# A dilated-convolution kernel: one written-out order of work replaced by another, with accumulating transfers placed differently around the loads

## The chip, the cores and the metric

The kernel runs on one core of one Trainium2 chip. The core has a matrix engine (PE, whose weight loads are listed as PEld), a vector engine (DVE), an activation engine (ACT), a general engine (POOL) and a synchronising engine (SP). SP and POOL also issue transfers, which run on 16 DMA engines. Each engine works through its own instructions in the order in which they were written and waits on semaphores for the others. The metric is the device time of one execution in microseconds (us).

## The reference

The input `x` has shape (2, 16000, 256). A causal convolution with three taps and dilation 2 makes 512 channels, the first 256 go through tanh, the other 256 through a sigmoid, their product is multiplied by a 256 x 256 matrix:

```
xp = jnp.pad(x, ((0, 0), (pad, 0), (0, 0)))          # pad = 4
h = einsum(xp[:, 4:4 + T], w[0])
for i in 1, 2:
    h = h + einsum(xp[:, 4 - 2*i : 4 - 2*i + T], w[i])
z = jnp.tanh(h[..., :256]) * sigmoid(h[..., 256:])
return z @ w_o
```

All inputs are bfloat16, as is the output (2, 16000, 256).

## The kernel before, in words

**Tiling.** Time is cut into 23 groups: one of kind P at the very beginning, 18 of kind A (6 time phases x 256 rows) and four of kind B (4 phases x 256 rows, the last of them 160 rows). A group is loaded by one transposing DMA (line 167, issued by SP), so that channels lie on the partitions. Of each group, four blocks of 128 output channels are worked out (`oi` 0 to 3). ORDER gives the sequence of the groups: three of kind B, then A, with the 160-row group last.

**The fast convolution.** Instead of three products for each output, an A group makes six output phases, two at a time, from five products, whose inputs are sums and differences of the phases. These inputs ("pre-sums") are made per group, 128 x 1024 elements each: `u0`, `u1`, `u2`, `e`, `f` from the loaded tile, `u3`, `uh`, `ud` as scaled copies of `u1`, and finally four that are added on top of one of those: `rp = f + u1`, `rm = e + u3`, `r0 = u0 + uh`, `ri = u2 + ud`. A B group needs only `m`, `p`, `d0`, `d3`. The weights are transformed to match; the pieces of the matrix `wa_sb` are made on POOL (line 233) in 16 steps, `wa.0` to `wa.15`: the first eight add into `wu`, the last eight write `wa_sb`. `wa.8` and `wa.12` serve block 0 of a group, `wa.10` and `wa.14` block 1, `wa.9` and `wa.13` block 2, `wa.11` and `wa.15` block 3; each needs the step numbered eight lower (`wa.9` needs `wa.1`, `wa.13` needs `wa.5`).

**Three ways to make a pre-sum.** On DVE in one piece (line 330 or 328); on POOL in four quarters (line 330, 128 x 256 each); or, for `rp`, `rm`, `r0`, `ri`, by a DMA that POOL issues (line 325) and that adds its source into its destination. Nearly all of those four kinds go by such an accumulating DMA, 67 in all.

**The order.** PLAN is a list of tokens, and each token writes one step; since each engine keeps its own order, the list sets the order on every engine at once.
- `F`, `M`, `L`, `Z`, `I`: the five products of the next block (line 359, two matmuls of 512 columns each): `F` uses `u1`, `M` uses `rm`, `L` uses `rp`, `Z` uses `r0`, `I` uses `ri` (for B groups `m`, `p`, `d0`, `d3`, and no `M`). `P` is the output product of one piece (line 478, four matmuls of 256 columns). `H` and `R` are its two halves for the last pieces. I call these, with the three `D`, the PE tokens.
- `c` copies the first product to SBUF on ACT (line 390). Behind `M` the second product is taken out of the accumulating bank by `h` (DVE, line 393) or by `k` (ACT, line 403). `A` and `Y` are combining sums on DVE (line 393). `b`, `y`, `a` are tanh or sigmoid on ACT (line 441), `g` the gate product on DVE (line 460).
- `e` and `v` take an output piece out of PSUM, on ACT (line 495) or DVE (line 487); `s` stores (line 504) and `x` loads the next group (line 167), both through SP's queue, in the list's order.
- `u1.3` makes that pre-sum of the fourth A group (they count from 0) on DVE; `u1.3q5` makes one quarter on POOL, held until the DVE step that was the fifth last at this point is done; `r0.3d` issues the accumulating DMA.

The first three groups (12 blocks) are of kind B, so the thirteenth `F`, the thirteenth `L`, the thirteenth `Z` and the first `M` belong to the first A group. Four loads are issued ahead of the list (lines 534 to 537), so the third `x` is the seventh load.

Of the kernel before, what the change touches and what calls it, by code (L numbers as in the profile page):

```python
# [40 lines left out]
f.8 e.7q127 c Z I Y y M b A rm.7d P a ud.8 rp.7d F k26 uh.7 Z u0.7 c I g y L r0.7d b M u2.7q72 A P a F k27 u3.8
u2.7q63 P Y e44 L c u1.9 ri.7d s17 I e45 s16 e.9 Z y x M A b P f.9 k28 P Y a F L e46 u2.8 Z e47 g I b u0.9q178 P c A
F e48 uh.8 M u0.9q158 c Y P a u0.9q136 h29 M y Z u0.8q109 h30 s18 I b rm.8d g L a L r0.8d y A F u0.9q4 e49 P Y I c
u3.9 Z a u1.10q52 A M b u2.9q181 Y I k31 F rm.9d uh.9 e50 e.10 Z c s19 L rp.8 b s6 P f.10q126 A x y M a F Y u2.9q45
P e51 h32 u2.9q161 Z c g u1.10q99 L b I y Y M y u1.10q83 F A a P u1.10q114 h33 c Z ri.8 rp.9d L b M ud.9 r0.9d y Y F
k34 I uh.10 u1.11q50 c A L a M v52 u1.11q37 e53 Z A f.10q162 k35 I y P Y u2.9q165 L a g x P e54 f.11q189 Z b A I e55
f.10q170 v56 F b P ri.9d Y c P u3.10 a F g s20 rm.10d y M s21 Z c h36 I e57 u0.10 M b L u2.10 a r0.10d F A k37 P
f.10q70 e58 Y L y P f.11q62 A c Z rp.10d ud.10 y P Y I ri.10d b u0.11 M e59 Z a h38 s22 F b x g L u1.12q10 c I e60 Y
M y P A u1.11q150 e61 F h39 u1.12q153 e62 Z e.11 c f.11q86 L I a Y M b u1.11q185 A P a f.11q166 F h40 y Z rp.11d
u3.11 c P uh.11 e63 rm.11d L f.12 b M g e64 I P k41 A u2.12q76 F a Y L u1.12q230 y I A c u2.12q102 Z a P u1.12q84 Y  # L50
b M u0.12 r0.11d e65 Z g rp.12d k42 F s24 I y s23 ud.11 L c u2.11 P b M e.12 ri.11d e66 P A k43 u1.13q10 F a v67 P
e68 L Y u1.13q109 c P A u1.13q60 Z e69 M e.13q198 e70 Y I b u2.12q181 h44 Z y F ud.12 a uh.12 L u3.12 c r0.12d P g b
M rm.12d e71 I Y u2.12q118 k45 F s26 A a P x u2.13 L c e.13q58 Z y A M b u1.13q162 I Y e72 F u0.13q202 h46 y P
ri.12d c f.13 Z a L u3.13 M u1.14 b P y A e.14q169 I k47 s25 g F e.13q265 e73 I a Y L c P e.13q147 A e74 Z u0.13q254
y M Y rm.13d P b uh.13 P h48 e75 rp.13d Z a ud.13 F f.14 b ri.13d L c g I e76 F u2.14q57 Y e77 M c P A s28 e.14q54 P
y x h49 u0.13q177 M a Z uh.14 u2.14q98 y h50 L b I u2.14q236 A y L e.14q154 Y a F P u2.14q72 e78 Y Z c u0.13q9 A I y
v80 M r0.13d b s27 I g e79 F k51 Z ud.14 c P e.15 a L u0.14 M b f.15q17 A P a P u3.14 k52 f.15q94 Y F e81 L e.14q63
v83 c Z y rp.14d A M b I g k53 P u2.15q37 F a Y L y ri.14d u1.15 I c rm.14d A Z e82 M r0.14d g b P e84 P h54 y F
u3.15 a L Y u1.16q196 P e85 Y rm.15d Z c I A y u2.15q160 M b v86 Z a e.16q217 h55 I s31 b F s29 g x L c F Y f.16q105
y P e87 A u2.15q23 M c P v88 f.15q32 a Z h56 u2.15q177 M b I uh.15 u1.16q75 e89 h57 L a F u1.16q59 A L c e.16q140 Y  # L60
P s30 y M f.15q111 A x y Z u1.16q79 Y k58 I rp.15d I b u3.16 u0.15 Z a F g b r0.15d L s32 c P e.16q208 A a P e90 M Y
f.16q60 y F ud.15 Z e91 u1.17 ri.15d I k59 u2.16 P b L u0.16 c F A e92 f.17q194 P c M s33 Y f.16q80 e93 P h60
f.16q78 a M g e94 Z rp.16d I b e.16q101 h61 L y P A a F d0.3q32 Y d3.3q94 e95 L f.17q110 P c s34 Y Z y f.17q31 A M b
rm.16d P h62 e96 Z f.17q256 y v98 I b F uh.16 g L a r0.16d I c d0.3q5 A F y M Y c d0.3q17 I rp.17q3 e97 h63 P a
# [582 lines left out]
```

## Time and profile before

| What | Value |
|---|---|
| Median of 3 runs | 261.07 us (260.9 to 262.49) |
| The profiled execution | 263.16 us, span 261.4 us |
| PE busy | 250.4 us (96%), 1428 matmuls |
| DVE busy | 244.4 us (93%) |
| ACT busy | 244.0 us (93%) |
| POOL busy | 176.2 us (67%) |
| Granted PE clock | 0.997 |
| Accumulating DMAs, issue to landing | 3.3 to 11.5 us, median 5.5 |
| Transposing loads, issue to landing | 4.6 to 14.1 us, median 8.6 |

The span is the time from the first to the last instruction of the profiled execution. A group of instructions is listed with its count, the busy time of all, the mean of one in ns, and behind a second bar the time in which its engine stood idle just ahead of it, with what ended most of that idle time. Rows of the timeline give the start, the duration, the engine, the line and the tile; a bracket gives the idle time ahead.

### The profile page before, as it was taken

The numbers are of one execution on the slowest core, as the hardware profiler recorded it, in microseconds if no ns is written. First come the engines' busy times: TensorE is split into PE (matmuls) and PEld (weight loads), VectorE is DVE, ScalarE is ACT, GpSimd is POOL, SyncE is SP. The second block draws the span as 40 slices with busy tenths as digits, with TensorE's granted clock in tenths as the row PEclk, the third lists the DMA queues.
The fourth block names the chain that finished last, engine by engine and source line by source line (L and its number), as shares of the span: only waits on it lengthen the run. The fifth ranks groups of instructions, "written<-read, shape, count | busy, mean of one in ns | idle before, by whom it ended". The sixth has DMA issues, their size and how long they took to land.

```text
span 261.4 us, 4573 instructions
## 1 busy us (share of the span) xinstructions
PE 250.4 (96%) x1428; PEld 138.0 (53%) x1428; DVE 244.4 (93%) x405; ACT 244.0 (93%) x490; POOL 176.2 (67%) x248
## 2 busy tenths in 40 slices
PE   8999986999999999999999999999999998999992
PEld 5654543554555645545545555555555554555681
DVE  2899996999999999999999999999999999999963
ACT  5988986999999999999999999999999999989992
POOL 1034884589859668975898798889688878792000
PEclk9999999999999999999999999999999999999998
DMA  6999999998997999999998999899979998275334
GB/s 194 187 208 196 157 154 237 260 203 171 190 242 187 193 203 302 191 219 236 235 268 164 273 195 255 173 215 244 244 146 233 209 227 208 48 182 170 122 128 166
DMA packets 84753, 52.52 MB, mean 201 GB/s; under 512 B 69080, under 2 KB 70360, under 8 KB 84728
## 3 DMA queue, kind: packets, MB, share of 16 engines
q1 hardware_dynamic: 74168, 33.71, 55.1%
q0 software_dynamic: 9648, 17.57, 40.4%
q10 hardware_dynamic: 912, 0.95, 1.1%
q8 instruction: 11, 0.18, 0.3%
q14 instruction: 14, 0.11, 0.1%
HBM read 1.25 MB, written 16.38 MB: 67 GB/s over the span
## 4 chain that ended last, share of the span: by engine, by line
PE 65%; DVE 16%; ACT 8%; issue 4%; DMA 4%; DVEq 0%; ACTq 0%
PE b L359 37%; PE o_ps L478 15%; PE a L359 9%; DVE a L393 5%; DMA u<-uh 4%; DVE zz L460 3%; ACT th L441 2%; ACT sg L441 2%; DVE yy L393 2%; ACT ss L390 2%; DVE u L330 2%; ACT osb L495 2%; PE b L379 1%; PE a L379 1%; PE a L149 1%
## 5 line engine op out<-in xcount | busy, mean ns | idle before, releaser
L478 PE MATMUL o_ps<-wo_sb,zz 128*128 128x256 bf16 x496 | 71.8, 273 | 0.2
L393 DVE SCALAR_TENSOR_TENSOR a<-ss,b 128x512 f32<-128x512 f32 (+1 forms) x88 | 59.6, 679 | 6.4 <-PE b L359 5.7
L495 ACT CAST osb<-o_ps 128x512 bf16<-128x512 f32 x101 | 62.9, 642 | 1.1 <-PE o_ps L478 0.9
L330 POOL TENSOR_TENSOR u<-xt 128x256 bf16<-128x256 bf16 x76 | 55.4, 744 | 11.5 <-PE b L359 7.7
L478 PEld LDWEIGHTS <-zz 128*128 128x128 bf16 x496 | 48.3, 98 | 27.6 <-DVE zz L460 0.8
L390 ACT COPY ss<-b 128x512 f32<-128x512 f32 (+1 forms) x88 | 54.3, 621 | 2.4 <-PE b L359 2.0
L359 PEld LDWEIGHTS <-w_sb 128*128 128x128 bf16 x352 | 34.1, 97 | 38.2 <-issue 3.6
L359 PE MATMUL b<-u,w_sb 128*128 128x512 bf16 x144 | 42.8, 379 | 2.9 <-DMA u<-uh 2.3
L359 PE MATMUL b<-f,wp_sb 128*128 128x512 bf16 x144 | 42.6, 379 | 0.9 <-DMA f<-u 0.7
L359 PE MATMUL a<-u,w_sb 128*128 128x512 bf16 x144 | 42.6, 379 | 0.9 <-DVE a L393 0.8
L359 PE MATMUL b<-u,wa_sb 128*128 128x512 bf16 x144 | 42.6, 379 | 0.4 <-ACT th L441 0.4
L359 PE MATMUL b<-e,wm_sb 128*128 128x512 bf16 x144 | 42.8, 379 | 0.0
L460 DVE TENSOR_TENSOR zz<-th,sg 128x1536 bf16<-128x1536 bf16 (+2 forms) x46 | 41.6, 907 | 0.0
L441 ACT ACTIVATE th<-b 128x512 bf16<-128x512 f32 (+1 forms) x44 | 27.8, 633 | 4.7 <-PE b L359 3.6
L330 POOL TENSOR_TENSOR e<-xt 128x256 bf16<-128x256 bf16 x32 | 25.8, 812 | 6.9 <-DVE a L393 3.4
L330 POOL TENSOR_TENSOR f<-xt 128x256 bf16<-128x256 bf16 x32 | 24.6, 778 | 7.1 <-PE b L359 4.0
L441 ACT ACTIVATE th<-a 128x512 bf16<-128x512 f32 (+1 forms) x44 | 28.0, 637 | 0.4 <-PE a L359 0.3
L441 ACT ACTIVATE sg<-a 128x512 bf16<-128x512 f32 (+1 forms) x44 | 28.0, 637 | 0.0
L441 ACT ACTIVATE sg<-b 128x512 bf16<-128x512 f32 (+1 forms) x44 | 27.7, 629 | 0.3
L393 DVE SCALAR_TENSOR_TENSOR hh<-ss,b 128x512 f32<-128x512 f32 x39 | 26.4, 680 | 0.5 <-PE b L359 0.4
L359 PEld LDWEIGHTS <-wp_sb 128*128 128x128 bf16 x176 | 17.1, 98 | 18.1 <-issue 2.1
L393 DVE SCALAR_TENSOR_TENSOR yy<-hh,b 128x512 f32<-128x512 f32 x39 | 26.3, 680 | 0.1
(68 smaller groups left out, 372.5 us busy)
## 6 DMA issues: line engine op xcount, KB each, us to landing
out_dram<-osb SPq DMA_DIRECT2D x36, 384.0 KB, 3.9
u<-uh POOLq DMA_DIRECT2D x18, 256.0 KB, 4.9
u<-ud POOLq DMA_DIRECT2D x17, 256.0 KB, 6.4
e<-u POOLq DMA_DIRECT2D x16, 256.0 KB, 4.2
f<-u POOLq DMA_DIRECT2D x16, 256.0 KB, 5.7
out_dram<-osb SPq DMA_DIRECT2D x8, 256.0 KB, 5.1
w_sb<-in_w_dram ACTq DMA_DIRECT2D x3, 256.0 KB, 4.1
xt<-in_x_dram SPq DMA_TRANSPOSE x22, 8.6
```

Of the source, the lines that this page charges most:

```text
L149: nc.tensor.matmul(wps[:], lhsT=ones[:, 0:P], rhs=ones, start=True, stop=True,)
L330: ins = eng.tensor_tensor(out=o, in0=a, in1=b, op=op)
L359: nc.tensor.matmul(G[bank, oi][:, :2 * R], lhsT=wmat[:, ct, osl], rhs=G[mv][:, :, ct, :R], start=which == "first" and ct == 0, stop=ct == ...
L379: nc.tensor.matmul(G[bank, oi][:, :4 * r].rearrange("p (j r) -> p j r", j=4), lhsT=w_taps[tap][:, ct, osl], rhs=xt[:, j0:j0 + 4, ct, c0 + ...
L390: nc.scalar.copy(out=G["ss", oi][:, :n], in_=G["b", oi][:, :n])
L393: return note(nc.vector.scalar_tensor_tensor(out=out, in0=in0, scalar=scalar, in1=in1, op0=ALU.mult, op1=op))
L441: nc.scalar.activation(out=G[name, dt][:, j:j + 2, :R], in_=G[bank, oi][:, :2 * R].rearrange("p (q r) -> p q r", q=2), func=(ACT.Tanh, ACT ...
L460: note(nc.vector.tensor_tensor(out=G["z"][:, dt, :, :n], in0=G["th", dt][:, :, :n], in1=G["sg", dt][:, :, :n], op=ALU.mult))
L478: nc.tensor.matmul(o_ps[:, q, :], lhsT=z, rhs=wo_sb[:, dt, :], start=dt == 0 and (q == 0 or len(dts) == NT), stop=dt == NT - 1, skip_group ...
L495: copy(out=G["osb", at][:, 2 * jp:2 * jp + 2, :], in_=o_ps[:])
```

## The change

Only the list PLAN changes. Counted by tokens:

| Step | Before | After |
|---|---|---|
| PE tokens of each kind, `c`, `A`, `Y`, `a`, `b`, `y`, `g`, `x`, `s` | | the same |
| second product on DVE (`h`) / on ACT (`k`) | 39 / 33 | 43 / 29 |
| output pieces on ACT (`e`) / on DVE (`v`) | 102 / 24 | 104 / 22 |
| accumulating DMAs | 67 | 67 (one fewer `r0` and `ri`, one more `rm` and `rp`) |
| `u0`, `u1`, `u2` whole on DVE / quarters on POOL | 35 / 76 | 31 / 92 |
| `e` whole on DVE / quarters on POOL | 10 / 32 | 13 / 20 |
| `rp` quarters on POOL | 4 | 0 |
| `d3` whole on DVE / quarters on POOL | 3 / 4 | 2 / 8 |
| `p` whole on DVE / quarters on POOL | 4 / 0 | 3 / 4 |
| all POOL quarters and weight steps together | 172 | 180 |
| of these held behind the very last DVE step (`q1`) | 13 | 21 |

The places of the accumulating DMAs and of the loads move: the third and the fourth `x` have 43 and 54 PE tokens ahead of them (before: 34 and 74). `rp.0` is no longer a DMA but a sum on DVE. `ri.0d` comes first, then `rm.0d`, then `r0.0d`, which stands right ahead of the fourth `x`. The diff, cut to its beginning and end:

```
 PLAN = """
-d0.0 m.0 d3.0 p.0 F F c G D c D L w L A D wa.7q2 F A wa.3q5 d Z c p.1 Z b d3.1 I b L m.1 a F d0.1 I wa.6q1 c F A a x
-L G c Z g I b f.0 P a L A e0 wa.4q1 P wa.1q1 A F I u1.0 c Z u2.0 a x L b u3.0 Z m.2 I wa.15q1 b F A a wa.12q12 P F
-uh.0 c g Z e1 L e.0 b I e2 A P rm.0d c x F d3.2 a rp.0d L p.2 e3 Z c d0.2 I b P A wa.14q1 a L u2.1 wa.9q27 e4 F A Z
-c wa.0q30 I g b wa.8q2 Z a L ud.0 wa.5q10 b I A F wa.2q13 a u1.1 F ri.0d c Z u0.0 c I u3.1 b L r0.0d u0.1 a P A s0 L
-wa.11q1 e5 F g wa.13q1 Z c A I wa.10q16 b M f.1 a Z u1.2 k0 P rp.1d b ud.1 F uh.1 L e6 e.1 u0.2q1 F c s3 A I c M
-u3.2 u0.2q18 a P Y k1 M rm.1d e.2 e7 Z ri.1d g k2 I L b r0.1d g P a A F e8 uh.2 L u1.3q42 c Y s4 P y s2 A M u1.3q24
-x e9 Z h3 u1.3q49 y P Y I b u0.2q39 L v10 a u1.3q47 F Y y u0.2q7 Z c A I r0.2d y P g Z b M u3.3 b F ud.2 k4 f.2 I c
...
-H H e122 g H s43 R R v123 R v124 e125 s44 s45
+p.0 m.0 d0.0 d3.0 F F c G D w D L c wa.1q1 F A wa.2q4 L c wa.7q5 Z A wa.4q4 I b d3.1 L a F d0.1 I m.1 c Z a A D
+wa.0q1 L x d p.1 wa.12q1 Z b A I b F G Z g c P b u1.0 F a I f.0 e0 L ud.0 a F u2.0 x P c u3.0 P wa.6q1 c A L e1
+d3.2q11 L A d3.2q12 Z I g b Z p.2 a I b m.2 F d3.2q1 P A c F ri.0d rp.0 a I e2 e.0 L e3 Z uh.0 c wa.14q1 P A b rm.0d
+P d0.2 e4 Z a g I s2 e5 F s0 u1.1 x b L u2.1 d3.2q1 P c A F a L u0.0 wa.10q34 c Z A I b wa.8q3 L u1.2 a Z uh.1 F b
+ud.1 wa.3q1 I A c F r0.0d g a x L c u0.1 Z e6 P u2.2 b M u3.1 I ud.2 k0 F g wa.5q1 a L A c P wa.13q47 e7 A Z
+wa.15q25 e8 M wa.11q2 Y b I wa.9q4 s3 k1 f.1 Z ri.1d a F e.1 L c g I rm.1d b M A rp.1d F k2 f.2 r0.1d P c Y P y M
+e.2 a L h3 e9 u1.3q1 Z A y I u1.3q3 L b Y P u1.3q27 a Y F e10 u1.3q55 I A c ri.2d Z e11 u3.2 M e.3 b rm.2d Z uh.2 y
...
+b I y g Z a F L v109 b P A a s39 P c Y F y I g c L a Z A L b P A e111 Z v112 I b I v113 y F Z c F g P c P a v114 a L
+L b A P e115 A P e116 g I Z v117 s41 a Z s40 b P b I v118 P a P e119 g H P v120 s42 R P e121 H e123 v122 H R s44 R
+e124 s43 e125 s45
```

More of the change, by code (lines that the diff above doesn't have):

```diff
@@ new lines @@
+e.2 a L h3 e9 u1.3q1 Z A y I u1.3q3 L b Y P u1.3q27 a Y F e10 u1.3q55 I A c ri.2d Z e11 u3.2 M e.3 b rm.2d Z uh.2 y
+rp.2d F g b P c u0.2 F k4 M f.3 r0.2d a I h5 c L u0.3q41 y P A rp.3d M a u0.3q46 L Y e12 P k6 Y Z y A I b L u3.3 e13
+I ud.3 rm.3d g a F Z c u1.4q17 A P y M u1.4q51 Y b P u1.4q77 v14 k7 Z a F e.4 s7 b L x g I c f.4q70 F y A M c
+u0.3q49 v15 P k8 M f.4q9 Y a L h9 f.4q61 e16 Z x e17 A f.4q44 P b L u1.4q53 Y I e18 uh.3 F a u2.4q73 Y Z c P u0.3q32
+A b I u2.3 r0.3d y Z u3.4 F y g rm.4d M b I c h10 F e19 u0.4 M a L h11 e.5q85 c P y A ri.3d P e20 L Y e.5q55 M a s9
@@ new lines @@
+Y I x k12 u2.4q96 A Z a P f.5 b L u1.5 e21 Z e22 F A I b u3.5 P c Y u2.5q56 F y g rp.4d M c Z u2.4q21 y h13 P b M
+uh.4 u2.5q32 a L h14 F e23 u2.5q18 Y I c s10 e.5q60 L A s8 a M u1.6q97 Y e24 P e.5q67 y h15 Z e25 I u2.4q35 A P b
+rp.5d e.6 L y r0.4d F g a Z c I uh.5 f.6q1 b A P a M ud.4 u2.5q107 e26 F Y P k16 ri.4d u0.5 s11 Z c g L r0.5d b P
+f.6q61 e27 A I y M v29 e28 P u2.6q119 Y a F u2.6q111 h17 P c rm.5d Z ud.5 y L u0.6 ri.5d b M A f.6q110 e30 P Y e31 F
+I h18 c u1.6q41 I e32 g M u2.6q35 a Z s13 a h19 x L b P u1.6q62 A L y f.6q34 Y F y I u1.6q22 A c Z u2.6q28 e33 Y P y
@@ new lines @@
+rp.6d e.7 P s12 b M g a Z F y h20 u0.7q138 I b u3.6 L c u2.7q95 F A e34 u2.7q119 P e35 Y M rm.6d c P s14 ud.6 a u1.7
+Z ri.6d k21 M uh.6 I b g r0.6d P e36 u2.7q79 L h22 a P e37 A F u2.7q30 y L Y u0.7q38 c P A e38 Z u0.7q22 y Y I s15 M
+b x ud.7 P u3.7 a e.8q13 h23 Z e39 F g b L c I A e.8q1 e41 F y Y M f.7q56 I c u1.8 rm.7d Z k24 x uh.7 M v40 b
+u0.8q38 L a h25 P f.7q64 y P A u0.7q84 e42 F Y P a L c f.8 f.7q1 Z e44 A I b e.8q8 Y M a F f.7q33 v43 k26 Z g c
+rp.7d I b L ri.7d ud.8 M a uh.8 r0.7d F y A P k27 u1.9 P u0.8q1 c Y L y M A u0.8q141 e45 Z y P Y e.8q10 I b e.9
@@ new lines @@
+rp.8d Z k28 f.9 F a I u3.8 b L g rm.8d c F e46 u0.8q94 A M c P h29 a u0.9q113 M Y e47 L u0.9q24 y P h30 s18 u2.9q173
+Z e48 s17 A I s16 r0.8d b Y x L e49 F g a Z u1.10q148 c P Y b M u3.9 u0.9q156 e50 A I y F u0.9q35 h31 Z a uh.9 L c
+e.10 I y f.10q121 A P a M u2.9q126 Y b P u1.10q64 h32 y Z s19 g y r0.9d P F e51 rp.9d ud.9 L b u2.8 P f.10q1 c F A x
+e52 I Y c f.10q61 M e53 ri.8 Z u1.10q41 a M h33 b I u2.9q193 h34 y L rm.9 F a P Y c u1.11q130 L e55 A u1.10q159 P y
+M A u2.9q40 e56 s20 Z Y I ri.9d b g Z k35 I ud.10 b F v54 L a u0.10 F s21 u1.11q1 c P x A c P uh.10 a f.11q177 M Y
@@ new lines @@
+e57 M f.10q205 h36 y Z k37 I u3.10 g L b u1.11q1 L e58 A F a P f.11q30 Y y I u1.11q125 A c Z a rm.10d P Y e59 M
+r0.10d e.11 b P s22 rp.10d u2.10 Z k38 I e60 g F b L u0.11 c u1.12q203 P e61 A M e62 F u2.11 u1.12q10 y P h39 c P
+f.11q159 Y P e63 M e64 uh.11 ri.10 Z a r0.11d L h40 b u1.12q70 P e65 A I y F Y s24 f.11q59 a L x v66 u1.12q202 Z c A
+I b M uh.12 a F u3.11 k41 Y I rm.11d c g L rp.11d y Z u2.12q144 y A P s23 P a Y M b ud.11 Z k42 f.12 ri.11d F e67 g
+L c u1.13q10 I b A M e68 P ud.12 u2.12q170 k43 Y F s25 a P x e.13q141 v69 L c u1.13q192 v70 Z y M A u1.13q56 b I h44
@@ new lines @@
+u1.13q143 y F y Y u2.12q33 P c L f.13 Z a u3.12 M e.12 b P k45 g I rm.12d e71 P u2.12q47 Y a L s26 y F A u2.13q9 P
+e72 A Z c ri.12d uh.13 I b ud.13 M Y e73 e.13q1 F a h46 Z rp.12d c I u0.12 b L g r0.12d M a F u2.13q107 A k47 P c L
+u3.13 u0.13q227 y Y I e74 M e.13q243 A e75 Z s27 e.14q133 h48 P b Y P e.13q204 y F f.14 rm.13d a Z g c L rp.13d I b
+u0.13q19 Y P e77 F A a M u2.14q139 v76 c Z e78 u0.13q220 h49 M s28 b I x u1.14 e.14q65 y L h50 F a e.14q155 A P y L
+c u0.13q34 Y I e79 A u2.13q15 M y Z Y e.14q244 a P g rp.14d b Z I k51 r0.13d uh.14 F e80 u3.14 L e.15 b P c A
@@ new lines @@
+f.15q119 F e81 ud.14 P u2.13q157 y Y M c u0.14 P ri.13d e82 Z u1.15 rm.14d k52 M g I a L b u2.15q51 h53 P a F A
+f.15q193 e83 L c u2.15q120 Y s30 P y s29 P A f.15q228 x y M Y u2.14q124 Z e84 h54 I u2.14q230 y Z g b f.15q1 L b F Y
+a I u2.14q32 c F A e85 P ri.14d u3.15 y M u1.16 r0.14d Z c h55 P b uh.15 M u0.15q1 a v87 I e86 F g u0.15q123 k56 L
+s31 c P x Y P y u0.15q60 A M e88 u2.15q270 L a h57 Z f.16q173 y A I b u2.15q92 L Y e89 P f.16q46 a Y F s32 u0.15q60
+Z A c rm.15d P b ud.15 I g y ri.15d M a F rp.15d h58 Z e90 r0.15d ud.16 I c u2.16 L b M e.16 e91 ri.16d F Y k59
```

49 lines of the change are left out of this document (7 added, 42 removed).

## The prediction

> **What bounds the kernel now.** I read the page's busy shares first, then the stages, then PE's waits.
>
> ```profile
> span 261.4 us, 4573 instructions
> PE 250.4 (96%) x1428; PEld 138.0 (53%) x1428; DVE 244.4 (93%) x405; ACT 244.0 (93%) x490; POOL 176.2 (67%) x248
> 30.00:45.00 15.00, 11.97 (x64) 5.96 (x63) 12.05 (x23) 11.44 (x23) 9.82 (x14) 1.00 1.22 177
> 45.00:60.00 15.00, 15.00 (x86) 8.21 (x85) 14.96 (x27) 14.95 (x31) 10.60 (x16) 1.00 1.11 224
> PE b L359 <- DMA u<-uh: 2.3, 1, 2.3
> PE a L359 <- DVE a L393: 0.8, 1, 0.8
> PE b L359 <- DMA f<-u: 0.7, 1, 0.7
> ```
>
> The stage rows give start and end, length, then busy time of PE, PEld, DVE, ACT and POOL, the granted clock, the DMA share and GB/s. From 45 to 60 us PE, DVE and ACT are all busy for 15 of 15 us: three engines share the load so evenly that moving a step among them buys little. From 30 to 45 us all three lose 3 us together. The waits say to what: PE stood 0.7 and 2.3 us behind accumulating DMAs, once each, and no other wait of PE reaches 1 us. So 3.0 us is what a better placing of these DMAs could win there, and PE's sum of work is unchanged.
>
> **Cover, and a test of it on the old list.** The list puts PE tokens between an accumulating DMA and the product that needs it. What one takes:
>
> ```profile
> 44.10 0.86 PE b L359 x4
> 52.34 0.87 PE o_ps L478 x8
> 25.61 1.19 POOL L325 DMA_DIRECT2D f<-u  x1
> L325 POOL DMA_DIRECT2D e<-u x1: 1010/1010/1010, 24.9 to 24.9; - x1
> L325 POOL DMA_DIRECT2D f<-u x1: 1193/1193/1193, 25.6 to 25.6; - x1
> DMA to landing us min/median/max: 5.2/8.3/11.5
> 32.25 0.86 POOL L325 DMA_DIRECT2D u<-uh  x1 [0.65 <-DVE u L330]
> DMA to landing us min/median/max: 9.9/9.9/9.9
> 37.13 0.60 PE L359 MATMUL b<-f,wp_sb 128*128 128x512 bf16 x2 [0.74 <-DMA f<-u]
> 42.20 0.60 PE L359 MATMUL b<-u,w_sb 128*128 128x512 bf16 x2 [2.30 <-DMA u<-uh]
> ```
>
> Four matmuls of 512 columns, that is two tokens, take 0.86 us, and eight output matmuls, two `P`, take 0.87: a PE token is 0.43 us. In the old list 25 tokens stand between `rp.0d` and its `L` (10.8 us); the answer for 25.61 holds two DMAs, `e<-u` of 24.9 with 5.2 us and this one with 11.5; 11.5 - 10.8 = 0.7, and PE waited 0.74. Between `r0.0d` and its `Z` stand 15 tokens (6.5 us); it took 9.9; 3.4, less the 0.7 already lost, is 2.7, and PE waited 2.30. So cover less landing time forecasts a stall to about 0.4 us, and I use it on the new list.
>
> **The DMAs of the first A group, and where the stall goes.** All 3.0 us come off. In the new list `rp.0` is a sum on DVE and cannot be late; `ri.0d` has 33 tokens (14.2 us), more than the longest landing of 11.5; `rm.0d` has 18 (7.7 us). But `r0.0d` has only 11 tokens to its `Z`: 4.7 us, against 6.5 before. It stands 11 tokens, 4.7 us, behind the third `x` and right ahead of the fourth. What an accumulating DMA takes some microseconds behind the start of a load:
>
> ```profile
> 169.37 6.29 SPq L167 DMA_TRANSPOSE xt<-in_x_dram  x1
> L325 POOL DMA_DIRECT2D u<-ud x1: 867/867/867, 171.8 to 171.8; - x1
> DMA to landing us min/median/max: 6.9/6.9/6.9
> 180.77 5.79 SPq L167 DMA_TRANSPOSE xt<-in_x_dram  x1
> L325 POOL DMA_DIRECT2D u<-uh x1: 882/882/882, 185.3 to 185.3; - x1
> DMA to landing us min/median/max: 4.5/4.5/4.5
> L325 POOL DMA_DIRECT2D e<-u x1: 866/866/866, 217.4 to 217.4; - x1
> DMA to landing us min/median/max: 3.3/3.3/3.3
> ```
>
> Behind loads it is 6.9 (2.4 us behind the start) and 4.5 (4.5 us behind), and the 9.9 above (6.2 us behind the load of 26.03, quoted below); 3.3 at 217.4, where no load is left. I take 6.9, the middle of the three, because the early stage is the fuller one but fewer DMAs are ahead of it here: a stall of 6.9 - 4.7 = 2.2 us, between 0 (4.5) and 6.8 (11.5).
>
> The Trainium skill, DMA: Bandwidth & Descriptors, section SWDGE vs HWDGE vs iDMA, says that transfers issued by GpSimd and by SP go into different queues inside each DMA engine and that the engine takes them in turn. By that rule a load slows an accumulating DMA throughout its flight and not only at its beginning, and an estimate of twice the 3.3 us would give 6.6 and a stall of 1.9 us instead of 2.2. The rule speaks against a distance from the beginning of loads being a remedy; the 9.9 us above is beyond it, so the trace agrees in direction only.
>
> `rm.1d` has 13 tokens (5.6 us; 17 before). Its nearest row:
>
> ```profile
> L325 POOL DMA_DIRECT2D e<-u x1: 880/880/880, 38.4 to 38.4; - x1
> DMA to landing us min/median/max: 7.1/7.1/7.1
> ```
>
> That is 1.5 us too long, but it is issued behind the stalled `Z` in the list with no `A` or `Y` between, so DVE and POOL run on and PE's 2.2 us at `Z` is cover for it: 0 beside that stall, 1.5 without it.
>
> **What is late next.** The third `F` of the first A group reads `wa.9`, which the old list made 21 tokens ahead, and `wa.13`, made seven ahead. Now five weight steps, `wa.5` to `wa.9`, stand between this `F` and the sixth PE token ahead of it.
>
> ```profile
> L233 POOL TENSOR_TENSOR wa_sb<-wu 128x128 bf16<-128x128 f32 x8 | 5.2, 653 | 2.4 <-DVE u L328 1.9 <-DVE d L330 0.3
> L233 POOL TENSOR_TENSOR wu<-wu 128x128 f32<-128x128 f32 x8 | 4.1, 524 | 16.0 <-ACT wu L227 11.8 <-DVE m L330 2.1 <-DVE f L330 2.0
> ```
>
> One of 0.52 and four of 0.65 are 3.1 us against six tokens, 2.6: 0.5 late, and `wa.5q1` is also held behind the gate product just ahead of it, up to 0.7 more. I take 0.9, from 0 to 1.2. It is the next PE token behind the `Z`, so beside a stall of 2.2 it costs nothing; without that stall it is what PE waits for.
>
> **Work moved among engines.**
>
> ```profile
> L393 DVE SCALAR_TENSOR_TENSOR hh<-ss,b 128x512 f32<-128x512 f32 x39 | 26.4, 680 | 0.5 <-PE b L359 0.4
> L403 ACT COPY hh<-b 128x512 f32<-128x512 f32 x33 | 21.3, 645 | 0.0
> L495 ACT CAST osb<-o_ps 128x512 bf16<-128x512 f32 x101 | 62.9, 642 | 1.1 <-PE o_ps L478 0.9
> L487 DVE CAST osb<-o_ps 128x512 bf16<-128x512 f32 x23 | 15.7, 683 | 0.3 <-PE o_ps L478 0.3
> L330 DVE TENSOR_TENSOR d<-xt 128x1024 bf16<-128x1024 bf16 x6 | 4.1, 687 | 0.0
> L330 POOL TENSOR_TENSOR u<-xt 128x256 bf16<-128x256 bf16 x76 | 55.4, 744 | 11.5 <-PE b L359 7.7 <-PE a L359 2.4
> ```
>
> DVE: four second products more, 4 x 0.680 = +2.7; two output pieces fewer, -1.4; one `d3` and one `p` fewer, two of about 0.69, -1.4; the other pre-sums cancel (three `e`, one `r0`, one `ri`, one `u1` more, three `u0`, two `u2`, one `rm` fewer). Together -0.1. ACT: -4 x 0.645 + 2 x 0.642 = -1.3. POOL: eight quarters more, 8 x 0.744 = +6.0 on 176.2 us busy of 261.4, so it has room. I take 0 for the three: ACT's -1.3 is no gain where PE and DVE are full beside it (bounds -1.3 and 0). POOL's quarters can be in VectorE's way:
>
> ```profile
> 131.98 1.43 DVE L460 TENSOR_TENSOR zz<-th,sg 128x1536 bf16<-128x1536 bf16 x1
> L460 DVE TENSOR_TENSOR zz<-th,sg 128x1536 bf16<-128x1536 bf16 x36 | 35.8, 995 | 0.0
> ```
>
> One gate product took 1.43 us where their mean is 0.995, 0.44 more. Eight quarters more, each with such a loss, are 3.5 us; but 36 of these products run among 172 POOL pieces and their mean leaves little room for it, so I take 0.2, from 0 to 3.5. The Trainium skill, SBUF — State Buffer, section Who interferes with whom, says that a VectorE instruction with two SBUF inputs and a GpSimd instruction that reads SBUF exclude each other for their whole length. The 1.43 agrees with it.
>
> **Later DMAs.** Over the whole list nine of the 67 have at most 13 tokens of cover (seven before) and 16 at most 15 (12 before). The old list's tight ones beyond 45 us cost PE nothing, by the waits above. I add 0.6 us for the new ones, from 0 to 3 (one stall as that of `r0.0` and one of 0.7).
>
> **The sum.** -3.0 + 2.2 + 0 + 0 + 0.2 + 0.6 = 0.0 us. Against the profiled execution of 263.16 us (span 261.4 and 1.8 around it) that gives 263.2; this execution lay 2.1 us above the median of 261.07, so the median after is 261.1, say 261.0. The forecast's own range is 259.6 to 262.6, with `r0.0` landing after 5.4 to 8.4 us.
>
> **Rival 1: the distance works.** `r0.0` lands within its cover, the old 3.0 us are gone and `wa.9` takes their place with 0.9; `rm.1` can take 1.5 of its own at the worst. For it: only three DMAs, not four, are issued up to and with `r0.0`, and the 4.5 us row. Against it: the two weakest covers of the early stage shrank. 261.07 - 3.0 + 0.9 = 259.0; with `wa.9` in time 258.1. Chance 0.28. If its weight steps are in time or ACT's 1.3 us tell as well, half of it, it is faster by more than 1%.
>
> **Rival 2, on the other side: two loads back to back.** The fourth `x` follows the third by 11 tokens, where 40 stood before.
>
> ```profile
> 21.68 4.16 SPq L167 DMA_TRANSPOSE xt<-in_x_dram  x1
> 26.03 7.70 SPq L167 DMA_TRANSPOSE xt<-in_x_dram  x1
> ```
>
> The old loads at 21.68 and 26.03 followed each other like that, and the DMA issued between them, at 25.61, is the one of 11.5 us. If `r0.0d`, which now stands at such a place, takes 11.5, PE waits 6.8 and the sum is 261.07 - 3.0 + 6.8 = 264.9. It decides from 10.3 us on (5.6 us of stall, over 1% slower). Against it: the DMA of 24.9 beside the same loads took 5.2, and the slow one had that one ahead of it in its queue. Chance 0.22.
>
> **Rival 3: collisions.** Of the POOL pieces 21, not 13, are released right behind the last DVE step, and collide with the next one: 3.5 us for the 0.2 in the sum, 264.4. Chance 0.05.
>
> **Numbers.** The forecast has 0.45. A measurement of this kernel can tell about 1%, 2.6 us: faster means under 258.5, slower over 263.7. Rivals 2 and 3 give 0.27 slower; half of rival 1, and 0.08 of the forecast's case, where the later order wins something too, give 0.22 faster; 0.51 lie within. The range goes from rival 1 with nothing late and half of ACT's 1.3, 258.1 - 0.6 = 257.5, to rival 2 with 0.6 of later stalls, 265.5.
>
> **What would show it.** In the new trace a wait of PE's line 359 for `u<-uh` at about 38 to 42 us, some 2 us long, with a landing of 6 to 8 us for that DMA: the forecast. No such wait, but one for `wa_sb` at the next token: rival 1. A wait over 5 us: rival 2. DVE's gate products with a mean above 1.05 us: rival 3. I am wrong altogether if the time is lost or won beyond 60 us by more than 2 us, because then the list's later order, which I costed only by its cover, decides.

## The result, and the profile after

| | Before | After |
|---|---|---|
| Median of 6 runs each, one chip | 260.99 us (260.71 to 262.49) | 259.34 us (259.15 to 259.45) |
| Ratio, 95% interval | | 0.9932 (0.991 to 0.9954) |
| Profiled execution, span | 263.16 us, 261.4 us | 259.23 us, 257.4 us |

The change makes the kernel 0.7% faster, 1.65 us. That lies within 1% and within the range; it is rival 1's number (259.0), not the forecast's (261.0). A second measurement on another chip, further down, gave 0.9933. Ratios and intervals leave out runs more than 1.5% above the fastest of the same kernel, which two kernels show, while medians and ranges hold every run.

The page of the kernel after, span and busy times (PLAN is one line longer, so every line number is one higher than before):

```profile
span 257.4 us, 4566 instructions
PE 250.3 (97%) x1428; PEld 137.8 (54%) x1428; DVE 242.4 (94%) x405; ACT 242.4 (94%) x488; POOL 179.5 (70%) x256
```

PE's work is the same to 0.1 us. DVE is busy 2.0 us less than the 244.4 before, though the count of its steps is the same and the steps that moved were worth 0.1 us. The step durations themselves fell, and that was the first hint.

PE's waits in the kernel after (us in all, times, longest):

```profile
PE a L150 <- PEq L632: 0.8, 1, 0.8
PE b L360 <- ACT ss L391: 0.4, 1, 0.4
PE b L360 <- DVE hh L394: 0.3, 1, 0.3
PE b L360 <- DMA u<-uh: 0.2, 1, 0.2
PE b L360 <- DMA e<-u: 0.2, 1, 0.2
```

No wait for a DMA reaches 0.3 us. The forecast wanted one of about 2 us here, for `u<-uh`. The one accumulating DMA that it spoke of, `r0.0d`, and what follows it, in the timeline of the kernel after and in the answer for its line:

```profile
34.14 0.87 POOL L326 DMA_DIRECT2D u<-uh  x1
...
37.95 1.70 POOL L234 TENSOR_TENSOR wa_sb<-wu 128x128 bf16<-128x128 f32 x4
39.51 0.59 PE L360 MATMUL b<-u,w_sb 128*128 128x512 bf16 x2
39.94 0.59 PE L360 MATMUL b<-u,wa_sb 128*128 128x512 bf16 x2
```

```profile
L326 POOL DMA_DIRECT2D u<-uh x1: 870/870/870, 34.1 to 34.1; - x1
DMA to landing us min/median/max: 5.2/5.2/5.2
```

It landed at 34.14 + 5.2 = 39.34 us and its `Z` began at 39.51. PE did not wait for it, with 0.2 us to spare. The four last weight pieces, `wa.9` among them, were done at 39.65, and the `F` that reads it began at 39.94. Nothing is late.

Where PE's time went, in the two stages that turn out to matter (start and end, length, busy PE, PEld, DVE, ACT, POOL, granted clock, DMA share, GB/s), after:

```profile
105.00:120.00 15.00, 14.71 (x82) 7.85 (x81) 14.86 (x26) 15.00 (x32) 12.71 (x18) 1.00 1.13 195
120.00:135.00 15.00, 15.00 (x85) 8.14 (x84) 15.00 (x26) 14.44 (x30) 13.07 (x19) 1.00 1.11 235
```

The same rows for the kernel before follow with the first experiment.

### The profile page after: what moved, and what is told of

The parts are those of the page before. It is cut to its first block, busy times and chain, and to the rows that moved or that the text cites. A ratio compares the mean times of both kernels' runs of the same rounds, so it can differ in the third digit from the quotient of the medians.

```text
span 257.4 us, 4566 instructions
## 1 busy us (share of the span) xinstructions
PE 250.3 (97%) x1428; PEld 137.8 (54%) x1428; DVE 242.4 (94%) x405; ACT 242.4 (94%) x488; POOL 179.5 (70%) x256
## 4 chain that ended last, share of the span: by engine, by line
PE 68%; DVE 9%; POOL 6%; ACT 6%; DMA 5%; issue 3%; ACTq 0%; DVEq 0%; POOLq 0%
PE b L360 40%; PE o_ps L479 14%; PE a L360 10%; DMA e<-u 3%; DMA u<-uh 3%; POOL f L331 2%; ACT sg L442 2%; DVE a L394 2%; DVE yy L394 2%; POOL u L331 2%; PE b L380 1%; PE a L380 1%; ACT osb L496 1%; ACT th L442 1%; ACT ss L391 1%
## 5 line engine op out<-in xcount | busy, mean ns | idle before, releaser
L331 POOL TENSOR_TENSOR u<-xt 128x256 bf16<-128x256 bf16 x92 | 70.1, 775 | 7.8 <-PE a L360 2.4
L479 PE MATMUL o_ps<-wo_sb,zz 128*128 128x256 bf16 x496 | 70.9, 273 | 0.0
L496 ACT CAST osb<-o_ps 128x512 bf16<-128x512 f32 x102 | 62.1, 626 | 0.8 <-PE o_ps L479 0.7
L391 ACT COPY ss<-b 128x512 f32<-128x512 f32 (+1 forms) x88 | 53.3, 608 | 1.1 <-PE b L360 0.6
L461 DVE TENSOR_TENSOR zz<-th,sg 128x1536 bf16<-128x1536 bf16 (+2 forms) x46 | 40.6, 884 | 0.0
L442 ACT ACTIVATE th<-b 128x512 bf16<-128x512 f32 (+1 forms) x44 | 26.9, 612 | 3.8 <-PE b L360 2.2
L394 DVE SCALAR_TENSOR_TENSOR hh<-ss,b 128x512 f32<-128x512 f32 x43 | 29.2, 680 | 1.0 <-PE b L360 0.9
L394 DVE SCALAR_TENSOR_TENSOR yy<-hh,b 128x512 f32<-128x512 f32 x43 | 29.1, 678 | 0.0
L442 ACT ACTIVATE th<-a 128x512 bf16<-128x512 f32 (+1 forms) x44 | 27.0, 615 | 0.4 <-PE a L360 0.3
L360 PEld LDWEIGHTS <-wm_sb 128*128 128x128 bf16 x176 | 17.0, 97 | 14.8 <-issue 1.0
```

Source lines behind the costliest of these rows:

```text
L331: ins = eng.tensor_tensor(out=o, in0=a, in1=b, op=op)
L360: nc.tensor.matmul(G[bank, oi][:, :2 * R], lhsT=wmat[:, ct, osl], rhs=G[mv][:, :, ct, :R], start=which == "first" and ct == 0, stop=ct == ...
L391: nc.scalar.copy(out=G["ss", oi][:, :n], in_=G["b", oi][:, :n])
L394: return note(nc.vector.scalar_tensor_tensor(out=out, in0=in0, scalar=scalar, in1=in1, op0=ALU.mult, op1=op))
L442: nc.scalar.activation(out=G[name, dt][:, j:j + 2, :R], in_=G[bank, oi][:, :2 * R].rearrange("p (q r) -> p q r", q=2), func=(ACT.Tanh, ACT ...
L461: note(nc.vector.tensor_tensor(out=G["z"][:, dt, :, :n], in0=G["th", dt][:, :, :n], in1=G["sg", dt][:, :, :n], op=ALU.mult))
```

## The experiments

The first theory was the prediction's own: the early DMAs decide. The rival was that the later order of the list does. Four runs were meant to tell them apart; two of them, the mixtures of the lists, could not.

**The kernel before, profiled once more.** No edit.

> The kernel before, unchanged, profiled once more. Its profiled execution took 263.16 us, 2.1 above the median. If the two waits for accumulating DMAs (0.7 and 2.3 us) belong to the list, they stand here again, together 2.5 to 3.5 us, and a profile near 261 us differs elsewhere. If they were an accident of that one execution, PE's waits for these DMAs are under 1.5 us together and the profile is near 260.7 to 261.1 us.

Measured: 260.99 us (259.99 to 261.47) where the kernel before had 260.52 on the same chip; the profiled execution took 260.83, span 259.0. PE's waits in it:

```profile
PE a L149 <- PEq L631: 0.8, 1, 0.8
PE a L359 <- DVE a L393: 0.7, 2, 0.5
PE b L359 <- ACT th L441: 0.4, 1, 0.4
PE a L359 <- DMA u<-ud: 0.4, 1, 0.4
```

The two waits of 2.3 and 0.7 us, on which the prediction rested, are not there. `rp.0d` was issued at 25.9 us (25.6 in the first profile) and landed after 7.2 us instead of 11.5, `r0.0d` after 5.4 instead of 9.9; their covers of 10.8 and 6.5 us hold that. So the median does not hold that stall. It was not unique, though: of the eight profiles here and below that have the old list's beginning, three show PE idle for 0.5 us or more between 30 and 45 us (3.4 in the first profile, 0.9 and 0.5 in two others), and five show under 0.1. A second loss stands in both profiles of the kernel before, from 105 to 135 us. Here is the second:

```profile
105.00:120.00 15.00, 14.58 (x80) 7.51 (x79) 15.00 (x27) 14.42 (x30) 10.31 (x14) 1.00 1.05 226
120.00:135.00 15.00, 14.17 (x73) 6.89 (x72) 14.71 (x25) 13.86 (x27) 13.25 (x18) 1.00 1.03 220
```

PE ran 80 + 73 = 153 matmuls in these 30 us, against 82 + 85 = 167 after. Matmuls are of two sizes, so I also took PE's idle time from the distance between the starts of matmuls, less the usual 0.216 us behind one of 512 columns and 0.109 behind one of 256. From 105 to 135 us that is 3.0 us here, 2.3 in the first profile and 1.0 in the kernel after.

**The new beginning with the old rest.** The new list up to its 80th PE token (about 45 us), then the remaining steps in the old order.

```
 PLAN:  p.0 m.0 d0.0 d3.0 F F c G D w D L ...  k4 | I c F ud.3 a L x c M ...
        (new list, 80 PE tokens)                  | (old order)
```

> The new list up to its 80th PE token (about 45 us), then all steps that are left in the order of the list before. Theory early: the gain lies in the first A group's DMAs, so this kernel has the whole gain, 259.0 to 259.7 us. Theory later: the gain lies in the order beyond 45 us, so this kernel stays at 260.5 to 261.3 us.

Measured: three runs from 274.01 to 274.28 us and one of 269.37, far slower than either list. At the seam a load comes early: in the new beginning the store that held SP's queue stands elsewhere, so the fifth `x` starts at 41.08 us, and three accumulating DMAs are issued 0.3 to 1.4 us behind its start. Timeline, and the answer for the DMA's line:

```profile
41.08 6.79 SPq L166 DMA_TRANSPOSE xt<-in_x_dram  x1
...
58.51 1.03 PE L358 MATMUL b<-e,wm_sb 128*128 128x512 bf16 x2 [9.53 <-DMA e<-u]
```

```profile
L324 POOL DMA_DIRECT2D e<-u x1: 859/859/859, 41.4 to 41.4; - x1
L324 POOL DMA_DIRECT2D f<-u x1: 1210/1210/1210, 41.9 to 41.9; - x1
L324 POOL DMA_DIRECT2D u<-uh x1: 1561/1561/1561, 42.4 to 42.4; - x1
DMA to landing us min/median/max: 17.1/18.1/18.7
```

The load itself landed after 19.8 us. PE stood 9.53 us, and its matmul behind that took 1.03 us instead of 0.59. The stages of this kernel show why:

```profile
50.00:55.00 5.00, 0.00 (x0) 0.00 (x0) 0.00 (x0) 0.00 (x0) 0.96 (x2) 0.74 1.24 90
55.00:60.00 5.00, 1.49 (x4) 0.58 (x5) 0.76 (x2) 0.36 (x1) 0.00 (x0) 0.50 1.39 71
```

All three engines stood, and the granted clock fell to 0.50 with the pause, which adds to the loss. This run says nothing on the first theory, but it shows the hazard that the change speaks of: DMAs too near to the beginning of a load.

**The old beginning with the new rest.** The old list up to its 81st PE token, then the remaining steps in the new order.

```
 PLAN:  d0.0 m.0 d3.0 p.0 F F c G D c D L ...  A I | u2.2 ud.2 f.2 P ri.2d e11 M ...
        (old list, 81 PE tokens)                   | (new order)
```

> The list before up to its 81st PE token (about 45 us), then all steps that are left in the order of the new list. Theory early: no gain, 260.5 to 261.3 us, with the waits for u<-uh near 42 us still there. Theory later: the whole gain, 259.0 to 259.7 us.

Measured: 260.14 us (259.56 to 263.02), ratio 0.9993 (0.9966 to 1.0021), between the two expectations. Its profiled execution took 259.79, and it has a wait at the seam that neither list has. Timeline, ACT:

```profile
47.34 0.59 ACT L495 CAST osb<-o_ps 128x512 bf16<-128x512 f32 x1 [1.98 <-DMA out_dram<-osb]
```

An output piece waited 1.98 us for a store that stands too late in this mixture, and PE stood 1.7 us behind it. The last run but one mends that.

**`rp.0` on DVE alone.** The change takes one of the two stalled DMAs away by making it a DVE sum; here that alone is done in the old list.

```
-... a rp.0d L p.2 ...
+... a rp.0 L p.2 ...
```

> The list before with one token changed: rp.0 is a sum on VectorE in place of the accumulating DMA issued at 25.6 us, which took 11.5 us. Theory queue: that DMA, caught behind the load of 26.0 us, held back the ones issued behind it; without it they land in 5 to 7 us, the waits of 0.7 and 2.3 us are gone, and the time is 258.5 to 259.8 us. Theory load: the load itself slows every accumulating DMA beside it, so u<-uh still takes 8 to 10 us, PE still waits about 2 us and the time is 260.3 to 261.5 us (VectorE's 0.7 us more comes on top).

Measured: 260.97 us (260.14 to 263.25), ratio 1.0032 (1.0008 to 1.0056). That is no gain but a loss of about 0.4 us: there was no lasting stall to take away. The number is the one expected of the theory that the load is to blame, but its mechanism is missing: `u<-uh` of 33.2 us landed after 3.6 us, and PE did not wait for it. PE's idle time in the first 30 us rose from 1.3 to 1.9 us.

The first theory has fallen: the old list does not usually lose 3 us at its beginning. What remained was the stretch beyond 100 us. I looked there for DVE steps longer than others of their kind. Timeline of the kernel before (second profile), DVE and the POOL pieces beside it:

```profile
102.34 2.65 POOL L330 TENSOR_TENSOR e<-xt 128x256 bf16<-128x256 bf16 x3
103.08 1.38 DVE L460 TENSOR_TENSOR zz<-th,sg 128x1536 bf16<-128x1536 bf16 x1
...
108.30 1.11 DVE L330 TENSOR_TENSOR f<-xt 128x1024 bf16<-128x1024 bf16 x1
...
113.27 0.76 DVE L328 TENSOR_SCALAR u<-u 128x1024 bf16<-128x1024 bf16 x1
...
124.14 0.88 DVE L328 TENSOR_SCALAR u<-u 128x1024 bf16<-128x1024 bf16 x1
...
128.40 3.76 POOL L330 TENSOR_TENSOR u<-xt 128x256 bf16<-128x256 bf16 x5
129.68 1.42 DVE L460 TENSOR_TENSOR zz<-th,sg 128x1536 bf16<-128x1536 bf16 x1
```

Undisturbed, these steps take 0.95, 0.68, 0.41, 0.41 and 0.95 us in the same stretch; five steps lose 0.43 + 0.43 + 0.35 + 0.47 + 0.47 = 2.15 us, each beside quarters on POOL. In the first profile the same steps take 1.38, 1.11, 0.77, 0.47 and 1.43: four of the five. What PE waited for from 105 to 135 us in the second profile (`issue`: no cause that the profile shows):

```profile
PEld L359 <- issue: 2.8, 8, 0.5
PEld L359 <- DVE hh L393: 0.8, 1, 0.8
PEld L478 <- DVE zz L460: 0.5, 1, 0.5
PE a L359 <- DMA u<-ud: 0.4, 1, 0.4
```

In the kernel after, the only wait for DVE listed there is one of 0.3 us, and `issue` has 1.4. So PE's waits for DVE shrink with DVE's longer steps, but much of its idle time has no named cause. The second theory: the old list loses about 2 us there, and the new one does not, because its quarters fall elsewhere. Its rivals: the distance of DMAs from loads, and the second products moved from ACT to DVE. Four kernels follow, of which two are on the distance.

**The hazard taken out of the mixture.** The mixture of the new beginning and the old rest, with one store moved ahead of that load.

```
-k4 I c F ud.3 a L x c M A P
+k4 I c F ud.3 a L s5 x c M A P
```

> The kernel of the new beginning and the old rest, which took 274 us because three accumulating DMAs issued at 41.4 to 42.4 us, right behind the start of a load at 41.1, landed after 17 to 18 us. Here one store moves: the one of pieces 9 and 10 goes ahead of that load in SP's queue, so the load starts at about 46 us. Theory distance: the three DMAs land after 5 to 7 us, PE's wait of 9.5 us is gone, and the time is 259.5 to 262 us. Theory seam: the loss comes from the seam between the two lists, not from the load, and the time stays over 268 us.

Measured: 261.65 us (261.3 to 262.16), ratio 1.0033 (1.0008 to 1.0059). Moving one token gives back 8 to 13 us (269.37 to 274.28 less 261.65, on two chips). The load starts at 47.44 us, behind the DMAs, which are issued at the same places in the list, the last of the three at 42.7 us:

```profile
L324 POOL DMA_DIRECT2D u<-uh x1: 1561/1561/1561, 42.7 to 42.7; - x1
DMA to landing us min/median/max: 5.5/6.3/7.1
```

And the new beginning, freed of the accident, gains nothing over the old one: the kernel before took 260.87 us on this chip.

**The hazard put into the new list.** The fifth `x` moved ahead of the store that held it.

```
-F e.4 s7 b L x g
+F e.4 x s7 b L g
```

> The new list with one token moved: the fifth load stands ahead of the store that held it in SP's queue until 57.2 us, and so starts as soon as its buffer is free, at about 41 us, beside the accumulating DMAs of 41.1 to 42.2 us. Theory distance: those DMAs take over 12 us and the time is 266 to 275 us. Theory seam: no effect, 259.0 to 260 us.

Measured: 267.37 us (264.66 to 268.28), ratio 1.0242 (1.0173 to 1.031). The load begins at 41.37 and lands after 15.7 us. The answer for the three DMAs behind it, with the last of them:

```profile
L325 POOL DMA_DIRECT2D u<-uh x1: 1563/1563/1563, 42.7 to 42.7; - x1
DMA to landing us min/median/max: 8.5/13.6/14.1
```

So a load that starts just ahead of several accumulating DMAs costs about 8 us (267.37 less 259.34): put in here, taken out in the run before. The Trainium skill, DMA: Bandwidth & Descriptors, section SWDGE vs HWDGE vs iDMA, has the two kinds of queue taken in turn, from which the prediction's estimate was 6.6 us; the 8.5 to 18.7 us of these six DMAs go beyond it.

**Fewer collisions in the old list.** Eight quarters (the expectation counts seven) are held behind the DVE step that they collided with. `q0` holds a quarter behind the very last DVE step written so far; `q1`, by the kernel's code, behind the one before that, and not behind the very last, as it is put ahead of the prediction.

```
-Z h23 e.8q119 s15 y P x g b e.8q1 L
+Z h23 s15 y P x g e.8q0 b e.8q0 L
-f.8 e.7q127 c Z
+f.8 e.7q0 c Z
-M u2.7q72 A P a F k27 u3.8 u2.7q63 P
+M A P a F k27 u3.8 u2.7q0 u2.7q0 P
-u3.9 Z a u1.10q52 A
+u3.9 Z a u1.10q0 A
-h32 u2.9q161 Z c g u1.10q99 L
+h32 Z c g u2.9q0 u1.10q0 L
```

> The list before; seven quarters that POOL ran while VectorE had a gate product, a pre-sum or a scaled copy to do between 103 and 131 us are held behind that VectorE step. In the list before five VectorE steps there took 0.35 to 0.47 us longer than their kind, 2.1 us together, and PE idled 3.1 us from 105 to 135 us. Theory collisions: the excess falls under 0.6 us, PE's idle time there to about 1.5, and the time by 1 to 2 us, to 258.6 to 259.8. Theory order: something else in that stage holds PE, and the time stays at 260.2 to 261.2 us.

Measured: 262.71 us (262.12 to 264.35), ratio 1.0085 (1.0052 to 1.0118): slower, the opposite of the edit's purpose. The groups of the scaled copies on DVE:

```profile
L327 DVE TENSOR_SCALAR uh<-u 128x1024 bf16<-128x1024 bf16 x18 | 9.6, 535 | 0.0
L327 DVE TENSOR_SCALAR ud<-u 128x1024 bf16<-128x1024 bf16 x18 | 9.2, 510 | 0.0
```

They had means of 489 and 467 in the second profile of the kernel before: the shifted quarters ran into other DVE steps. I summed, over all DVE steps, what each takes above the median of its kind (operation and shape), where that is more than 0.03 us: 5.7 us for the kernel before (second profile), 7.7 here, 3.6 for the kernel after. The edit had made more collisions, and 1.8 us of time went with 2.0 us of them. It missed its aim and so does not test the place, but the price agrees with the theory.

**Four second products back on ACT.** In the new list the extra four `h` are `k` again.

```
-h10 ... h19 ... h31 ... h34
+k10 ... k19 ... k31 ... k34
```

> The new list with four of its second products (10, 19, 31, 34) taken by ScalarE again, as in the list before, so 39 on VectorE and 33 on ScalarE. By the prediction's term of 0 for work moved among engines: 259.0 to 259.8 us, as the new list. If the four on VectorE are what the new list gains by, the time is 260.2 to 261 us.

Measured: 260.04 us (259.68 to 260.65), ratio 0.9974 (0.9953 to 0.9994). That is 0.7 us above the kernel after (by the ratios, since the two were measured on different chips, 1.1 us), between what the two theories gave. The sum above the median is 4.3 us here, 0.7 more than after, so the loss may again be collisions (the steps behind them shift) rather than ACT's load; this run doesn't separate the two.

Then the collisions themselves, without moving anything.

**Eleven POOL quarters as zeros, beside the five steps.** In the old list the quarters at 102 to 131 us are written with zeros instead of being summed, at the same places in the list. The kernel leaves these sums out, so the outputs of their groups are not the reference's.

```
+    BLANK = {("e.8", 0), ("e.8", 1), ("e.8", 2), ("e.7", 3), ("u2.7", 2), ("u2.7", 3), ...
...
+        if (token, had) in BLANK:
...
+            hold(settle(nc.gpsimd.memset(quarter, 0.0), True), behind)
+            return
```

> The list before; the eleven quarters that POOL ran beside the five lengthened VectorE steps from 103 to 131 us only fill their place with zeros, so POOL reads nothing there (these parts of four pre-sums are left out, and the outputs of their groups are not the reference's). Theory collisions: VectorE's excess over the kernel, 5.7 us in the last profile of this list, falls by about 2, PE's idle time from 105 to 135 us falls from 3.1 to about 1.5, and the time by 1 to 2 us, to 0.992 to 0.996 of the list before. Theory order: the stage is held by something else, the ratio is 0.998 to 1.002.

Measured: 259.3 us (258.36 to 260.68), ratio 0.9924 (0.9896 to 0.9953) to the kernel before. Stages:

```profile
105.00:120.00 15.00, 15.00 (x88) 8.26 (x87) 15.00 (x28) 15.00 (x32) 9.19 (x14) 1.00 1.08 220
120.00:135.00 15.00, 14.92 (x78) 7.45 (x77) 14.78 (x26) 14.70 (x30) 12.59 (x20) 1.00 1.13 252
```

88 + 78 = 166 matmuls, about as many as the new list had, and 0.8 us of idle time by the distances. The five steps are back at 0.94, 0.68, 0.41, 0.42 and 0.95 us, and the sum above the median is 3.6 us. Of PE's waits for DVE one of 0.2 us is left in that stretch, and `issue` has 1.4.

**The same number of zeros elsewhere.** The control: the eleven quarters at 136 to 165 us.

> The control: the list before, with eleven quarters from 136 to 165 us, where VectorE shows no lengthened step, filled with zeros in the same way (parts of six pre-sums left out, those outputs are not the reference's). Theory collisions: no change, ratio 0.998 to 1.002. If less work on POOL helps wherever it is, 0.992 to 0.996.

Measured: 261.9 us (260.28 to 268.08), ratio 1.0016 (0.9979 to 1.0053). It shows no gain, but as a control it is not clean. Its profiled execution took 264.0 us, and PE waited in it for DMAs issued at 137.9 and 154.8 us:

```profile
PE a L359 <- DMA u<-ud: 1.5, 1, 1.5
PE b L359 <- DMA e<-u: 1.3, 1, 1.3
```

A load started at 132.75 us here, 0.3 us behind an accumulating DMA, and at 137.23 in the kernel before. From then on the accumulating DMAs took 9.0 to 12.0 us for 30 us, where they took 4.5 to 7.5 in the same stretch of the kernel before. So a gain from less work on POOL may be covered up by these stalls. What speaks against such a gain is the lowest run: 260.28 us, against 260.01 for the kernel before and 258.36 with the zeros beside the five steps. That the place of the eleven quarters matters, and not the amount of POOL's work, is therefore likely and not settled by this pair.

The zeros are also shorter than the sums (0.31 us against 0.67), so the pair doesn't say by itself whether the loss is the collision or the length of the POOL pieces. In the kernel before nothing in the stretch waited 0.2 us or more for a sum on POOL except POOL's own DMA issues (0.3 us, twice). One of these leads on to PE: the DMA `u<-ud` for which PE waited 0.4 us was issued 0.4 us earlier with the zeros, and the wait was gone. So of the 2.2 us of idle time that the zeros take away some 0.4 may be the length of POOL's pieces; for the rest it is the five DVE steps that were longer.

**The old beginning, its store mended, with the new rest.** `s2` moved ahead of `s3` in the mixture of the third run.

```
-F c s3 A I c M ... Y s4 P y s2 A M
+F c s2 s3 A I c M ... Y s4 P y A M
```

> The old beginning with the new rest, where an eviction waited 2.0 us at 47 us for a store that stood late in SP's queue. That store (of the first half of the second B group) moves ahead of the next one. If the new list's gain lies beyond 45 us and the seam's store cost it 2 us, this kernel takes 258.0 to 258.8 us, under both lists. If the gain needs the new beginning, it stays at 259.8 to 260.6 us.

Measured: 258.98 us (258.82 to 259.51), ratio 0.9914 (0.9882 to 0.9946) to the kernel before, 260.85 on this chip. This version is faster than both kernels, 0.45 us below the new list on the same chip (259.43, next run). All of the gain lies beyond 45 us, and the new beginning adds none. It costs something: in the first 30 us PE's idle time is 2.2 us in every kernel with the new beginning and 1.3 in those with the old one (1.9 with `rp.0` on DVE, which the new list has too). That is enough for the 0.45 us.

The sum above the median is 4.4 us here, 0.8 more than the new list's, and the kernel is no slower for it. But a longer DVE step costs time only where PE needs it. From 102 to 135 us alone, with the same two measures:

| Kernel | DVE above the median, us | PE idle, us |
|---|---|---|
| before, second profile | 2.14 | 3.02 |
| `rp.0` on DVE | 1.72 | 2.34 |
| new beginning, hazard taken out, old rest | 1.67 | 2.25 |
| eight quarters moved | 3.02 | 3.13 |
| zeros elsewhere | 2.13 | 3.06 |
| zeros beside the five steps | 0.00 | 0.81 |
| after | 0.45 | 1.02 |
| old beginning, new rest (both versions) | 0.45 | 1.00 |
| new list, four products back on ACT | 1.23 | 1.26 |

In this table every kernel with the old rest and its sums beside these steps is above 1.6 and 2.2 us, and every one with the new rest unchanged is at 0.45 and 1.0. The last row doesn't fit as well: 0.8 us more on DVE went with only 0.2 us more on PE.

**The kernel after, once more on that chip.**

> The changed kernel unchanged, beside the three others on one chip: 259.0 to 259.7 us, with all runs within 0.5 us of each other, since no accumulating DMA is issued within 0.3 us of a load's start except one that has over ten microseconds of cover. A spread over 1.5 us as that of the list before would speak against the spread being a matter of these places.

Measured: 259.43 us (259.27 to 259.57), ratio 0.9933 (0.9905 to 0.996). Its nine runs spread over 0.3 us, the 26 of the kernel before over 3.8 (260.01 to 263.85).

## Why the prediction was right, and where it was wrong

The range and the expectation of a change within 1% held; the working did not, and the number was near by luck. The 259.34 us lie just outside the forecast's own range of 259.6 to 262.6, and two terms that nearly cancelled were both absent. Step by step:

- **"All 3.0 us come off."** Wrong. There were not 3.0 us in the median to come off: the stall comes in some executions only, as the second profile shows. The sign was in the text: the profiled execution "lay 2.1 us above the median", and I still subtracted a wait that made most of that excess from the median.
- **A stall of 2.2 us at `r0.0d`.** Wrong, 0 measured. It landed after 5.2 us, not 6.9; and its cover was 39.51 - 34.14 = 5.4 us rather than 4.7, because POOL issued it ahead of PE's place in the list. The two errors, -3.0 and +2.2, nearly cancelled, and that is why the sum of 0.0 was not far off.
- **Cover less landing time forecasts a stall.** This arithmetic held: 7.2 against 10.8, 5.4 against 6.5 and 5.2 against 5.4 us, no wait in any. What limits it is the landing time, which differed by 4.3 and 4.5 us between two executions of the same kernel.
- **`wa.9`, 0.9 us late.** Not late. The four pieces took 1.70 us together, 0.46 each, where I had taken the old list's mean of 0.65.
- **`rm.1`, 0.** Held: it landed after 5.2 us of 5.6 us of cover.
- **Work moved among engines, 0.** Not settled: the run with four products back on ACT lost 0.7 to 1.1 us of the 1.65, through ACT's load or through the collisions that the edit shifted.
- **Collisions, "0.2, from 0 to 3.5".** The step that failed. I had costed only collisions that the change adds. I quoted one gate product of 1.43 us in the old list, and took from a mean of 0.995 that there was little of this. I left out the bound below nothing: that the new list may lose fewer than the old. It does: the means of the gate product fell from 993 to 970 ns, of `uh` from 489 to 441, of `ud` from 467 to 421, of `f` from 736 to 697, and DVE's sum above the median from 5.7 to 3.6 us, by 2.1. The eleven zeros show that the old list loses about 1.5 us (260.85 less 259.3) to POOL's quarters at this one place, by their collisions and in a smaller part perhaps by their length. That the new list's gain is the same 1.5 us is argued from the place (beyond 45 us, by the old beginning with the new rest) and from DVE's and PE's times in that place (the table above); it is not shown by putting the collisions back into it. What was off in the prediction is a term bounded below by 0 that, by this argument, came out at about -1.5.
- **Rivals.** Rival 1's number came true without its cause: there was no old stall that the distance could remove, and `rp.0` on DVE alone brought nothing. Rival 2, two loads back to back, did not come: `r0.0d`, 0.4 us ahead of a load, took 5.2 us, and 4.5 in the second profile of the kernel after. Its mechanism is real all the same: `rp.0d` at such a place took 11.5 us in the first profile of the kernel before and 7.2 in the second, and the moved load cost 8 us or more. What makes it strike in one execution and not in another stays open. Rival 3 named the right resource with the wrong sign (and `q1` holds behind the last DVE step but one, so its 21 pieces are not released where it says).
- **"I am wrong altogether if the time is lost or won beyond 60 us by more than 2 us."** That is what happened. PE's idle time, taken from the distance between matmuls in the second profile of the kernel before and in that of the kernel after, fell from 6.5 to 4.1 us between 60 and 240 us, 2.0 of it from 105 to 135. In the first 30 us it rose from 1.3 to 2.2. Together that is 1.5 us, and the medians differ by 1.65.

What stays open: the steadiness of the new list (0.3 us of spread) may come from the distance of its DMAs from loads, but the old beginning with the new rest is nearly as steady (0.7 us), so it would have to be the later DMAs; no run tries that. And what in the new beginning leaves PE idle for 0.9 us more in the first 30 us is shown only in part: `rp.0` on DVE alone adds 0.6.

## What to carry to other kernels

Profile a kernel twice before pricing a stall that one execution shows, above all when that execution lies above the median: a transfer that was late once may be in time in most executions. Where three engines are busy together, compare the longest step of each kind with its usual one: the mean of a kind hides five steps that cost 2 us, and what a new order takes away can be worth as much as what it adds. A load starts when SP's queue lets it, so its distance from other transfers is set by the stores ahead of it, and moving one store can be worth 8 to 13 us. A control changes more than it is meant to, so read its waits too before leaning on its time.

## What the runs showed of the hardware

**Transfers that start together.** Accumulating DMAs of 256 KB took 3.3 us at best and 5.5 in the median in the first profile of the kernel before. They took 8.5 to 18.7 us when three of them were issued 0.3 to 1.4 us behind the start of a transposing load, and the load itself took 15.7 to 19.8 (median before: 8.6). While this lasted the DMA engines were busy (share 1.24 to 1.39 in the stages above) and moved 90 and 71 GB/s, where the page of the kernel after has a mean of 204. Coming ahead of the load did not always protect them: one issued 0.4 us ahead of a load took 5.2 and 4.5 us in the two profiles of the kernel after, but 11.5 in the first profile of the kernel before, with 14.1 for the load. Where one or two were issued up to 1.4 us behind a load's start, in the other profiles, they took 5.6 to 10.8 us. In the control one issued 0.3 us ahead took 12.0, and a load 14 us later 18.5.

**What on POOL slows DVE.** Sums of two tiles on POOL lengthened DVE's two-input steps (0.95 to 1.42 us) and its one-input scaled copies (0.41 to 0.88); zeros written in their place did not (0.94 and 0.42). The sums got longer too: three that are 0.67 us each undisturbed took 2.65 us beside a gate product. The Trainium skill, SBUF — State Buffer, section Who interferes with whom, says that a VectorE instruction with two SBUF inputs contends with a GpSimd instruction that reads SBUF and not with one that only writes it; the zeros agree. That scaled copies are hit too agrees with what it says there of the two-port modes of `tensor_scalar`.
